# Attention and two gated layers on one core: the first batch's heads in another order, its loads and copies spread over engines, other paces, and idle products on TensorE

## The chip, the cores and the metric

The kernel runs on one core of a Trainium2 chip (trn2). The metric is the device time of one execution in microseconds. The core's engines are TensorE (PE, its weight loads are PEld), VectorE (DVE), ScalarE (ACT), GpSimd (POOL) and SyncE (SP), which issues most DMAs.

## The reference

```python
def _attn_ref(q, k, v):                       # 4 batches, 8 heads, 576 rows, 64 columns
    scores = scale * np.matmul(q, k.transpose(0, 1, 3, 2))
    rel = pos[:, None] - pos[None, :]
    mask_local = (rel >= 0) & (rel < 32)      # heads 0 to 3
    mask_strided = (rel >= 0) & (pos[None, :] % 32 == pos[:, None] % 32)   # heads 4 to 7
    ...
    return np.matmul(softmax(scores), v)

def _moe_ref(x, w_gate, w_val, w_out, rms_g): # x: 2304 x 512, w_gate and w_val: 512 x 1536
    xn = x / sqrt(mean(x * x) + 1e-6) * rms_g
    g = xn @ w_gate
    return (g / (1 + exp(-g)) * (xn @ w_val)) @ w_out
```

The heads of the attention are joined to x (2304 x 512), `_moe_ref` follows with its scale by the root mean square, and a second layer of the same kind without that scale ends it. All arrays are float32.

## The kernel before, in words

**Attention.** A batch (`batch`, L606) is cut into ten groups, each with scores, softmax, a turn of the probabilities and the product with v. Five are *strided* (heads 4 to 7, rows of equal remainder modulo 32, 126 or 108 rows to a group), five are *local* (heads 0 to 3, windows of 64 queries with 96 keys). q and k are loaded with rows on the partitions (`load`, L267) and must be turned on PE (`strided_t`, `local_t`, `local_rest`) before scores can be made; PSUM results are copied to SBUF by ACT, or with `eng()` (L236) by DVE once in a hundred. The local q is written into a zeroed tile `qT`, two heads on a block diagonal (`diagonal`, L316); POOL sets that tile to zero (L310). In `softmax_step` DVE takes the masked row maximum (L397, tile `e` with its maximum `nb`), ACT the exponential (L406), DVE the reciprocal `rc` (L417), and POOL multiplies (L423).

**The way to the first layer.** Outputs go to `x`: ACT squares them, DVE adds the squares to `ss` (`squares`, L535). `rms_step` (L556) sums `ss` over partitions on PE with a tile of ones, DVE takes the mean, POOL the power -0.5 (`rstd`, L576), DVE puts it on a diagonal (`dg`, L581), PE spreads it to all partitions (L587), DVE scales x (L592). Each batch has two parts, of 256 and 320 rows. `split_x` splits x into a rounded part `xh` (ACT) and the rest `xl` (DVE).

**The gated layers.** A product of two float32 matrices is three products of such parts. For each of 12 chunks of the inner dimension there are a gate, a value and a down product (`gate`, `down`). The first layer runs over seven blocks of tokens with chunks 0 to 5, one with all, then the rest (`segs`, L775). Weights come as float32 in 512 KB loads into three buffers (`raw`, L163) and are split by six operations a half kilobyte wide: on ACT L173, L174 and L187, on DVE L180, L181 and L192. Six chunks have 18 such loads, so 54 operations on ACT and 54 on DVE.

**What sets the order.** The program calls `point()` at fixed places: in a loop ahead of the first layer, and behind every half of a gate, value or down product. Each point moves all started steps on by a phase and then starts new ones by `pace`: so many attention steps (`att`) and weight steps (`dec`) to a point. A scheduler then orders each engine's instructions by priorities; every engine runs its own list in order. Ahead of the first layer PE's banks are shared by eight tags, later the attention has two, `a0` and `a1`.

```python
    pace.update(att=1.0)
    for i in range(1000):
        if (0, 0) in att.done:
            break
        pace["dec"] = 0.7 if i >= 0 else 0.0
        point()
```

Ahead of the first layer batch 0 is computed: all strided turns first, then the strided groups, then the local ones; its first scale is started behind the seventh group, its second behind the tenth. The attention of batch 1 is started between the products of the first two token blocks.

Of the kernel before, what the change touches and what calls it, by code (L numbers as in the profile page):

```python
# [25 lines left out]
def attn_ffn_ffn(ctx: ExitStack, tc: tile.TileContext, q, k, v, w1g, w1v, w1o, rms_g, w2g, w2v, w2o, out):  # L26
# [179 lines left out]
    class Attention:  # L206
# [29 lines left out]
        def eng(self):  # L236
            self.turn += 1
            return nc.scalar if self.turn % 100 else nc.vector

        def consts(self):  # L240
# [5 lines left out]
            for m, lead in ((self.m0, 0), (self.m1, 32)):  # L246
                g.memset(m, 0.0)
                for par in range(2):
                    sel(m[64 * par:64 * par + 64], [[-1, 96]], lead, 1)
                    sel(m[64 * par:64 * par + 64], [[1, 96]], 31 - lead, -1)  # L250
# [7 lines left out]
        def load_strided(self, t, src, b, engs=None):  # L258

            engs = engs or [nc.sync] * 5  # L260
            for h in range(HH):
                s = src[b, HH + h].rearrange("(t r) d -> t r d", r=32)[:, 0:30, :].rearrange("t (a g) d -> a t (g d)", g=5)
                engs[h].dma_start(out=t[0:108, h].rearrange("p (g d) -> p g d", d=D), in_=s)  # L263
            s = src[b, HH:H].rearrange("h (t r) d -> t h r d", r=32)[:, :, 30:32, :].rearrange("t h r d -> t h (r d)")
            engs[4].dma_start(out=t[108:126, :, 0:2 * D], in_=s)

        def load(self, b, half):  # L267
            res = []
            for nm, src in (("q", q), ("k", k)):
                if half == 0:  # L270
                    t = self.p1.tile([128, 5, HH * D], F32, tag=nm, name=f"{nm}n{b}{half}")
                else:
                    t = self.p1.tile([126, HH, 5 * D], F32, tag=nm, name=f"{nm}n{b}{half}")
                    self.load_strided(t, src, b, [nc.sync,nc.sync,nc.gpsimd,nc.gpsimd,nc.sync] if b == 0 and nm == "k" else None)
                res.append(t)
            self.ld[b, half] = res
            if half == 0:
                for h in range(0, HH, 2):
                    for t, src in zip(res, (q, k)):
                        for h_ in (h, h + 1):  # L280
                            nc.sync.dma_start(out=t[:, 0:4, h_ * D:(h_ + 1) * D], in_=src[b, h_, 0:512].rearrange("(c p) d -> p c d", p=128))
# [59 lines left out]
        def local_rest(self, b):  # L341
# [9 lines left out]
            def post():  # L351
# [4 lines left out]
                if b + 1 < B:  # L356
                    self.load(b + 1, 1)
# [557 lines left out]
```

## Time and profile before

| | us |
|---|---|
| median of 3 runs | 1068.74 (1063.17 to 1069.88) |
| the profiled execution | 1067.38 |
| its span, first to last instruction | 1065.6 |
| PE busy | 1036.2 (97%) |
| DVE, ACT, POOL busy | 463.8, 438.2, 58.4 |
| moved by DMA | 100.39 MB, 94 GB/s on average |

The profiled execution is one run of the program with the hardware profiler on; durations below are of this execution. Its mean granted TensorE clock was 0.973 of full speed. A busy PE is not PE at its best: at half clock it is as busy and does half the work.

### The profile page before, as it was taken

What the parts mean: (1) busy time and instruction counts of PE and PEld (TensorE: products, weight loads), DVE (VectorE), ACT (ScalarE), POOL (GpSimd) and SP (SyncE); (2) the same over time, 40 slices, a digit from 0 to 9 for tenths busy, and PEclk for the clock granted to TensorE, in tenths of its full rate; (3) what the DMA queues carried; (4) which work ended last, traced back from release to release, by engine and by line L of the source; (5) the groups of instructions that cost most, each with busy time, mean ns of one, the idle gap of its engine ahead of it and who ended that gap; (6) DMA issues with size and microseconds to landing.
All of it is one profiled execution on the core that took longest, in us unless ns stands there. A gap on an engine that the chain in (4) does not pass through costs nothing.

```text
span 1065.6 us, 15758 instructions
## 1 busy us (share of the span) xinstructions
PE 1036.2 (97%) x6056; PEld 912.0 (86%) x6056; DVE 463.8 (44%) x1152; ACT 438.2 (41%) x1082; POOL 58.4 (5%) x83
## 2 busy tenths in 40 slices
PE   4988999999999999999999999999999999999998
PEld 4768999999999999988888898888888888888887
DVE  3788446355455861762313586222224313222212
ACT  5987546645635751651211565222124312212111
POOL 3312102102100000000000000000000000000000
PEclk9658999999999999999999999999999999999999
DMA  7794142243024630642123375111112003030202
GB/s 196 191 242 152 62 124 84 73 113 76 26 77 155 220 132 2 203 165 73 40 60 94 105 249 176 39 40 40 40 40 92 8 1 108 1 99 1 79 1 90
DMA packets 104261, 100.39 MB, mean 94 GB/s; under 512 B 40565, under 2 KB 92477, under 8 KB 103545
## 3 DMA queue, kind: packets, MB, share of 16 engines
q1 hardware_dynamic: 103992, 99.10, 30.2%
q8 instruction: 48, 0.79, 0.3%
q0 software_dynamic: 192, 0.28, 0.1%
q14 instruction: 29, 0.23, 0.1%
HBM read 77.47 MB, written 21.89 MB: 93 GB/s over the span
## 4 chain that ended last, share of the span: by engine, by line
PE 91%; DMA 3%; ACT 3%; DVE 2%; SPq 1%; issue 1%; DVEq 0%; ACTq 0%
PE b_y L63 28%; PE b_a L63 27%; PE b_v L63 17%; PE b_g L63 16%; PE b_a L66 2%; DMA xf<-x_d 1%; SPq L263 1%; DMA raw<-in_moe_w_val_dram 1%; DMA raw<-in_moe_w_gate_dram 1%; ACT e L406 1%; ACT dh L173 0%; DMA raw<-in_moe_w_out_dram 0%; ACT x L73 0%; DVE x L592 0%; DVE dr L180 0%
## 5 line engine op out<-in xcount | busy, mean ns | idle before, releaser
L63 PE MATMUL b_a<-xh,w 128*128 128x512 f32 (+3 forms) x816 | 231.4, 359 | 0.0
L63 PE MATMUL b_g<-xh,w 128*128 128x512 f32 (+3 forms) x696 | 192.6, 342 | 0.7 <-DVE sg L665 0.7
L63 PE MATMUL b_v<-xh,w 128*128 128x512 f32 (+3 forms) x696 | 192.4, 341 | 0.0
L63 PEld LDWEIGHTS b_a<-xh,w 128*128 128x128 f32 x816 | 147.4, 188 | 21.5
L63 PE MATMUL b_y<-hh,w 128*128 128x320 f32 (+3 forms) x624 | 165.1, 329 | 0.0
L675 ACT CAST hh<-sg 128x512 fp32r<-128x512 f32 (+3 forms) x138 | 72.6, 526 | 203.8 <-DVE sg L674 181.4
L63 PE MATMUL b_a<-xl,w 128*128 128x512 f32 (+3 forms) x408 | 146.6, 359 | 0.0
L63 PEld LDWEIGHTS b_g<-xh,w 128*128 128x128 f32 x696 | 125.3, 191 | 13.8 <-DVE sg L665 0.9
L63 PEld LDWEIGHTS b_v<-xh,w 128*128 128x128 f32 x696 | 124.8, 190 | 12.7 <-issue 0.7
L63 PE MATMUL b_y<-w,hh 128*128 128x512 f32 x432 | 133.2, 390 | 0.0
L63 PEld LDWEIGHTS b_y<-hh,w 128*128 128x128 f32 x624 | 110.0, 188 | 8.1 <-issue 0.7
L63 PE MATMUL b_g<-xl,w 128*128 128x512 f32 (+3 forms) x348 | 116.9, 336 | 0.0
L63 PE MATMUL b_v<-xl,w 128*128 128x512 f32 (+3 forms) x348 | 116.5, 335 | 0.0
L674 DVE TENSOR_TENSOR sg<-sg,b_v 128x512 f32<-128x512 f32 (+3 forms) x51 | 31.2, 611 | 167.6 <-PE b_v L63 163.9
L676 DVE TENSOR_TENSOR hl<-sg,hh 128x512 fp32r<-128x512 f32 (+3 forms) x138 | 80.8, 585 | 47.6 <-ACT hh L675 46.7
L674 DVE TENSOR_TENSOR sg<-sg,b_a 128x512 f32<-128x512 f32 (+3 forms) x51 | 31.2, 611 | 160.1 <-PE b_a L63 160.0
L63 PE MATMUL b_y<-hl,w 128*128 128x320 f32 (+3 forms) x312 | 100.8, 323 | 0.0
L63 PEld LDWEIGHTS b_y<-w,hh 128*128 128x128 f32 x432 | 80.4, 188 | 16.2
L667 ACT ACTIVATE sg<-b_a 128x512 f32<-128x512 f32 (+3 forms) x51 | 27.3, 536 | 144.8 <-PE b_a L63 144.7
L63 PEld LDWEIGHTS b_a<-xl,w 128*128 128x128 f32 x408 | 76.8, 188 | 10.9
L63 PE MATMUL b_y<-w,hl 128*128 128x512 f32 x216 | 84.0, 389 | 0.0
L667 ACT ACTIVATE sg<-b_g 128x512 f32<-128x512 f32 (+3 forms) x51 | 27.4, 537 | 121.7 <-PE b_g L63 121.7
(124 smaller groups left out, 1294.6 us busy)
## 6 DMA issues: line engine op xcount, KB each, us to landing
raw<-in_moe_w_gate_dram SPq DMA_DIRECT2D x24, 512.0 KB
raw<-in_moe_w_val_dram SPq DMA_DIRECT2D x24, 512.0 KB
raw<-in_moe_w_out_dram SPq DMA_DIRECT2D x24, 512.0 KB
xf<-y_d SPq DMA_DIRECT2D x5, 1024.0 KB
out_dram<-ob SPq DMA_DIRECT2D x18, 256.0 KB
xf<-x_d SPq DMA_DIRECT2D x8, 512.0 KB
part<-ob SPq DMA_DIRECT2D x14, 256.0 KB
ob<-part SPq DMA_DIRECT2D x14, 256.0 KB
```

Source lines behind the costliest of these rows:

```text
L63: traced(nc.tensor.matmul(out_, a, b_, start=start, stop=stop))
L66: traced(nc.tensor.transpose(out_, a, one))
L263: engs[h].dma_start(out=t[0:108, h].rearrange("p (g d) -> p g d", d=D), in_=s)
L406: r = nc.scalar.activation(out=e[:qn, i, :kn], in_=e[:qn, i, :kn], func=AF.Exp, bias=nb[:qn, i:i + 1], scale=-1.0, accum_out=sums[:qn, i:i ...
L667: last["act"] = ins_of(nc.scalar.activation(out=s[:, :n], in_=pg[:, :n], func=AF.Silu))
L674: nc.vector.tensor_tensor(out=s[:, :n], in0=s[:, :n], in1=pv[:, :n], op=ALU.mult)
L675: last["act"] = ins_of(nc.scalar.copy(out=hh[:, :n], in_=s[:, :n]))
L676: last["dve"] = ins_of(nc.vector.tensor_tensor(out=hl[:, :n], in0=s[:, :n], in1=hh[:, :n].bitcast(F32), op=ALU.subtract))
```

## The change

- **Loads.** For batch 0 the local q and k are loaded first, q by SP and k by ACT's queue, each in one 512 KB load in which a partition holds four neighbouring rows of a head, plus a load of the last 64 rows. Later batches take the same row order with four loads as before. Local v of a batch is loaded in two DMAs in place of nine, and a window's look-back for the first window comes from the head before it, where the mask hides it; `m0` and `kT` have 32 columns more of padding for that. A strided tensor is loaded in seven DMAs of 18 partitions and four heads, in place of four of 108 partitions and one of 18; none is issued by POOL now. One weight load is issued among the first strided loads.
- **Order.** Batch 0 has local groups before strided ones. Its strided turns are started after three groups, its strided q and k have tiles of their own (in weight buffers of chunks not yet loaded). Both scales of batch 0 stand behind all ten groups. The loads of batch 1 follow the strided turns of batch 0.
- **Turning.** In batch 0 the local q and k are turned by products with the identity (64 output rows, one head each), eight to a bank in place of four transposes.
- **Copies.** Ahead of the first layer `eng()` gives copies to DVE and ACT in turn. The first `qT` is zeroed by DVE.
- **Idle products.** `warm(n)` makes n products of ones with the identity into a bank that nobody reads: 8 behind the sums of the first scale, 12 behind its spreading.
- **Paces.** Ahead of the first layer `dec` is 0.25 a point, with one weight step started at once; in the layer `att` is 0.35, 1.1, 0.7, 0.7, 0.65 by blocks, where it was 0.7, 0.7, 0.65.

```diff
         def eng(self):
             self.turn += 1
-            return nc.scalar if self.turn % 100 else nc.vector
+            return nc.vector if state["start"] and self.turn % 2 else nc.scalar
...
+        def load_strided(self, t, src, b, eng):
+            rows = src[b, HH:H].rearrange("h (t r) d -> t h r d", r=32)
+            for a in range(6):
+                eng.dma_start(out=t[18 * a:18 * a + 18], in_=rows[:, :, 5 * a:5 * a + 5, :].rearrange("t h r d -> t h (r d)"))
+            eng.dma_start(out=t[108:126, :, 0:2 * D], in_=rows[:, :, 30:32, :].rearrange("t h r d -> t h (r d)"))
...
+                eng = nc.scalar if b == 0 and i and not half else nc.sync
...
+                    eng.dma_start(out=m_.rearrange("p (h c) -> p h c", h=HH), in_=src[b, 0:HH, 0:512].rearrange("h (p c) d -> p h (c d)", c=4))
...
-                    nc.gpsimd.memset(t, 0.0)
+                    (nc.gpsimd if b else nc.vector).memset(t, 0.0)
...
+                    if b == 0:
+                        for par in range(2):
+                            product(tp[64 * par:64 * par + 64, 128 * c:128 * c + 128], src[0][:, c, 2 * pair + par, :], self.ident,
+                                    start=True, stop=True)
+                    else:
+                        turned(tp[:, 128 * c:128 * c + 128], src[0][:, c, 128 * pair:128 * pair + 128], self.ident)
...
+        def warm(self, n):
+            t = self.abank()
+            for _ in range(n):
+                product(t[:, 0:128], self.ones, self.ident, start=True, stop=True)
...
             def mean():
+                if b == 0 and part == 0:
+                    self.warm(8)
...
             def post():
+                if b == 0 and part == 0:
+                    self.warm(12)
...
+            if b == 0:
+                groups = groups[5:] + groups[:5]
...
+            if b == 0:
+                res += [self.rms_step(b, part) for part in range(2)]
...
+    att.load(0, 0)
+    wq += [weight_step(m, c, z) for m, c in order for z in range(3)]
+    att.load_v(0, 0)
+    start(wq.pop(0))
     att.load(0, 1)
     att.load_v(0, 1)
...
-        pace["dec"] = 0.7 if i >= 0 else 0.0
+        pace["dec"] = 0.25
...
-        pace["att"] = (.7,.65,.65)[min(si // 2, 2)]
+        pace["att"] = (.35, 1.1, .7, .7, .65)[min(si, 4)]
```

PE's list from the sums of the first scale (`ones,ss`) to the first gate product (`b_g<-xh`); `dg,ones` is the spreading of a scale, `ident,qn` and `ident,kn` are turns of batch 1, `kT,qT` its first scores. Before:

```order
L63 MATMUL b_y_806<-ones,ss 128x1 x2
L66 MATMUL b_a_891<-ident,qn_492 128x108 x4
L63 MATMUL b_g<-dg,ones 128x128 x2
L63 MATMUL b_a_896<-ones,ss 128x1 x2
L63 MATMUL b_a_896<-ones,ss 64x1
L66 MATMUL b_a_901<-ident,kn_498 128x108 x4
L66 MATMUL b_a_913<-ident,qn_492 64x108 x4
L66 MATMUL b_a_923<-ident,kn_498 64x108 x4
L63 MATMUL b_a_941<-kT_889,qT_882 126x126 x4
L63 MATMUL b_g<-xh,w_0_0_207 128x256
```

and of the changed kernel the same stretch:

```order
L63 MATMUL b_a_780<-ones,ss 128x1 x2
L63 MATMUL b_g<-ident,ones 128x128 x8
L66 MATMUL b_a_875<-ident,qn_362 128x108 x4
L63 MATMUL b_a_884<-ones,ss 128x1 x2
L63 MATMUL b_a_884<-ones,ss 64x1
L63 MATMUL b_v<-dg,ones 128x128 x2
L63 MATMUL b_y_814<-ident,ones 128x128 x12
L66 MATMUL b_a_889<-ident,kn_370 128x108 x4
L66 MATMUL b_a_905<-ident,qn_362 64x108 x4
L66 MATMUL b_a_917<-ident,kn_370 64x108 x4
L63 MATMUL b_a_936<-kT_873,qT_865 126x126 x4
L63 MATMUL b_g<-xh,w_0_0_225 128x256
```

The eight idle products stand ahead of the spreading, the twelve behind it, with three turns and four scores of batch 1 between them and the gate.

DVE's list from the diagonal of the first scale (`dg`) to the first `xl`; `dr`, `dh` and `w` are weight operations, and the rows with `gcol` scale x. Before:

```order
L581 TENSOR_SCALAR dg<-ident,rstd 128x128 x2
L553 TENSOR_TENSOR ss<-ss,sq 128x320
L181 SCALAR_TENSOR_TENSOR dh<-dh,dr 128x512
L192 TENSOR_TENSOR w_2_2_455<-dh,w_2_2_455 128x512
L592 SCALAR_TENSOR_TENSOR x_761<-x_761,gcol,b_g 128x256 x2
L592 SCALAR_TENSOR_TENSOR x_413<-x_413,gcol,b_g 128x256 x2
L180 SCALAR_TENSOR_TENSOR dr<-raw,dr 128x512
L573 TENSOR_SCALAR mean<-b_a_896 64x1
L573 TENSOR_SCALAR mean<-b_a_896 128x2
L192 TENSOR_TENSOR w_3_0_485<-dh,w_3_0_485 128x512
L180 SCALAR_TENSOR_TENSOR dr<-raw,dr 128x512
L689 TENSOR_TENSOR xl<-x_761,xh 128x256 x2
```

and changed:

```order
L628 TENSOR_SCALAR dg<-ident,rstd 128x128 x2
L180 SCALAR_TENSOR_TENSOR dr<-raw,dr 128x512
L181 SCALAR_TENSOR_TENSOR dh<-dh,dr 128x512 x2
L192 TENSOR_TENSOR w_3_0_737<-dh,w_3_0_737 128x512
L620 TENSOR_SCALAR mean<-b_a_884 64x1
L620 TENSOR_SCALAR mean<-b_a_884 128x2
L180 SCALAR_TENSOR_TENSOR dr<-raw,dr 128x512
L641 SCALAR_TENSOR_TENSOR x_448<-x_448,gcol,b_v 128x256 x2
L641 SCALAR_TENSOR_TENSOR x_679<-x_679,gcol,b_v 128x256 x2
L192 TENSOR_TENSOR w_3_1_777<-dh,w_3_1_777 128x512
L628 TENSOR_SCALAR dg<-ident,rstd 128x128 x2
```

Between the diagonal and the scaling of x stand five weight operations now, where there were two.

POOL's list of batch 1's strided groups (126 and 108 rows), with the memset of that batch's `qT`. Before:

```order
L423 TENSOR_TENSOR e<-e,rc 126x4x126
L310 MEMSET qT_1193 128x2304
L423 TENSOR_TENSOR e<-e,rc 126x4x126
L423 TENSOR_TENSOR e<-e,rc 108x4x108 x3
L423 TENSOR_TENSOR e<-e,rc 128x4x96 x4
```

and changed:

```order
L457 TENSOR_TENSOR e<-e,rc 126x4x126 x2
L457 TENSOR_TENSOR e<-e,rc 108x4x108 x2
L330 MEMSET qT_1316 128x2304
L332 MEMSET kT_1360 128x32
L457 TENSOR_TENSOR e<-e,rc 108x4x108
```

The memset has moved from behind the first group to behind the fourth.

## Rows read from the trace of the kernel before

**Rows 1.** The page's 40 slices: PE's busy tenths, the granted clock's tenths.
```profile
PE   4988999999999999999999999999999999999998
...
PEclk9658999999999999999999999999999999999999
```

**Rows 2.** Four stretches of the span: busy us of each engine (instructions).
```profile
core 0: us, PE busy (x) PEld busy (x) DVE busy (x) ACT busy (x) POOL busy (x), PEclk, DMA share, GB/s
0.00:69.45 69.45, 48.94 (x317) 39.12 (x317) 45.47 (x157) 55.13 (x168) 20.44 (x39) 0.70 0.82 211
69.45:100.00 30.55, 26.97 (x155) 24.27 (x155) 25.08 (x85) 23.15 (x73) 7.38 (x6) 0.72 0.68 196
100.00:1000.00 900.00, 898.96 (x5251) 795.32 (x5251) 378.24 (x885) 350.27 (x821) 30.54 (x38) 1.00 0.26 85
1000.00:1065.60 65.60, 61.34 (x338) 53.29 (x336) 14.99 (x27) 9.61 (x20) 0.00 (x0) 1.00 0.16 56
```

**Rows 3.** PE in order of time: start us, us, instruction, [idle before <- releaser].
```profile
8.69 1.07 PE L66 MATMUL b_a<-ident,qn 126*128 126x126 f32 x4 [8.69 <-DMA qn<-in_q_dram]
...
60.03 1.22 PE L63 MATMUL b_g<-dg,ones 128*128 128x128 f32 x4 [1.23 <-DVE dg L581]
61.05 1.15 PE L63 MATMUL b_a<-ones,ss 128*128 128x1 f32 x6
...
67.45 2.07 PE L63 MATMUL b_a<-kT,qT 64*126 64x126 f32 x8 [0.65 <-ACT qT L73]
69.45 0.58 PE L63 MATMUL b_g<-xh,w 128*128 128x256 f32 x1
...
90.38 1.10 PE L66 MATMUL b_a<-ident,e 126*126 126x126 f32 x4 [2.21 <-POOL e L423]
```

**Rows 4.** Five stretches of PE: length, busy (instructions), granted clock, DMA.
```profile
69.45:82.90 13.45, 13.45 (x57) 0.50 0.89 232
82.90:88.30 5.40, 5.26 (x42) 1.00 0.79 256
88.30:90.40 2.10, 0.02 (x1) 0.84 0.54 191
90.40:93.20 2.80, 2.80 (x14) 0.51 0.01 3
93.20:100.00 6.80, 5.44 (x46) 1.00 0.51 157
```

**Rows 5.** DVE in order of time: the first maximum, the first xl.
```profile
16.02 0.29 DVE L397 CUSTOM_DVE_ANT_0 e<-b_y,ms 126x126 f32<-126x126 f32 x1 [16.02 <-PE b_y L63]
...
65.45 0.75 DVE L689 TENSOR_TENSOR xl<-x,xh 128x256 fp32r<-128x256 f32 x2
```

**Rows 6.** The stretch between these two, columns as in rows 2.
```profile
16.02:65.45 49.43, 39.78 (x268) 31.22 (x265) 41.47 (x147) 46.65 (x153) 14.89 (x15) 0.62 0.91 220
```

**Rows 7.** SP's first issues, and two stretches (columns as in rows 2).
```profile
0.74 3.30 SPq L263 DMA_DIRECT2D qn<-in_q_dram  x4
...
8.00:12.00 4.00, 2.22 (x10) 1.88 (x11) 0.00 (x0) 0.61 (x2) 0.00 (x0) 1.00 0.43 148
16.00:20.00 4.00, 1.76 (x28) 1.59 (x25) 3.58 (x30) 3.09 (x13) 2.02 (x1) 1.00 1.14 340
```

**Rows 8.** DVE groups to 110 us (busy, mean), and L180: min/median/max ns.
```profile
L75 DVE COPY qT<-b_a 64x512 f32<-64x512 f32 x3 | 2.1, 694 | 0.1
L75 DVE COPY qT<-b_a 64x128 f32<-64x128 f32 x1 | 0.3, 295 | 0.3 <-ACT qT L73 0.3
...
L180 DVE SCALAR_TENSOR_TENSOR dr<-raw,dr x18: 675/688/1395, 18.2 to 93.8; 128x512 uint32<-128x512 uint32 x18
```

**Rows 9.** POOL in order of time, batch 1's memset and what follows.
```profile
87.32 2.02 POOL L310 MEMSET qT<- 128x2304 f32 x1 [8.34 <-PE b_a L63]
89.30 3.20 POOL L423 TENSOR_TENSOR e<-e,rc 126x504 f32<-126x504 f32 x3
```

More of the change, by code (lines that the diff above doesn't have):

```diff
@@ L373, in post @@
                 o = (0, 504, 936)[part]
-                copy(self.eng(), self.qk_tile(b, 1, which)[:m, o:o + 4 * n], cell["t"][:m, 0:4 * n])
+                copy(self.eng(), self.strided_qk(b, which, o, 4 * n)[:m], cell["t"][:m, 0:4 * n])
                 self.count(b, 1)
-                if last:
+                if last and b:
                     self.load(b, 0)
-                    if b == 0:
-                        self.load_v(0, 0)
+                elif last:
+                    self.load(1, 1)
             return Step([pe, post])
@@ L506, in mms @@
                     o = self.SOFF[g] + h * n
[L507 removed]
+                    product(bank_[:n, 128 * h:128 * h + n], self.strided_qk(b, 0, o, n)[row], self.strided_qk(b, 1, o, n)[row],
+                            start=True, stop=True)
                 return bank_
@@ L547, in squares @@
                     x = self.x_tile(b, 0)
-                    rest = [(x[:, a, o:o + n], self.ss[b][:, o:o + n]) for a in range(2)]
+                    if b == 0:
+                        nc.scalar.activation(out=ss[:, o:o + n], in_=x[:, 0, o:o + n], func=AF.Square)
+                    rest = [(x[:, a, o:o + n], ss[:, o:o + n]) for a in range(int(b == 0), 2)]
                 for xa, sa in rest:
@@ L600, in store @@
                 self.done.add((b, part))
-            return Step([wait] * 3 + [pe1, mean, diag] + [wait] * 1 + [bc, post, store], lambda: (b, part + 1) in self.sq and (not part or (b, 0) in self.done), PRIO_R, "r")
+            return Step([wait] * 3 + [pe1, mean, diag] + [wait] * 1 + [bc, post, store], lambda: {(b, 0), (b, part + 1)} <= self.sq and (not part or (b, 0) in self.done), PRIO_R, "r")
         TILES = [tuple((p, j) for j in js) for js in ((0, 1, 2, 3), (4, 5, 6, 7)) for p in range(2)] + [((0, 8), (1, 8))]
@@ L798, in attn_ffn_ffn @@
     make_identity(nc, att.ident)
+    att.load(0, 0)
+    wq += [weight_step(m, c, z) for m, c in order for z in range(3)]
+    att.load_v(0, 0)
+    start(wq.pop(0))
     att.load(0, 1)
     att.load_v(0, 1)
-    wq += [weight_step(m, c, z) for m, c in order for z in range(3)]
-    for _ in range(0):
-        start(wq.pop(0))
     att.consts()
```

127 lines of the change are left out of this document (70 added, 57 removed).

## The prediction

> **What bounds the kernel now.** I read the page first, then the windows over the whole span, then the start in finer views. The page [rows 1] shows TensorE at 9 tenths or more in all but the first four slices, and in exactly these the granted clock is 9, 6, 5 and 8 tenths. The four stretches [rows 2] say it in numbers: from 100 us to 1000 us PE stands idle 900.00 - 898.96 = 1.04 us at clock 1.00, and in the last 65.60 us it idles 4.26 us on the way of the last results. So from 100 us on the time is TensorE's own work, which the change hardly touches, and only what lies before 100 us can be won or lost.
>
> The first product of the gated layers starts at 69.45 us [rows 3]. Between there and 100 us PE gets through less work than it could, in two ways [rows 4]. 13.45 us run at clock 0.50, the lower of the two levels (1.2 GHz), and 2.80 us more at 0.51: at 2.4 GHz these would be 6.73 and 1.40 us. And PE idles: 0.14, 2.08 and 1.36 us. In work at the full clock the stretch holds 6.73 + 5.26 + 0.02 + 1.40 + 5.44 = 18.85 us in 30.55 us, so 11.70 us are lost, 8.1 of them to the clock and 3.6 to waits.
>
> If F is the time at which the first gate product starts, this gives one formula for the new span: F + 18.85 + 965.60 + r = F + 984.45 + r, where r is what is still lost behind F. Before it is 69.45 + 984.45 + 11.70 = 1065.6, the span. The profiled execution took 1067.38 us, 1.78 more than its span, and 0.13% under the median of the three runs, 1068.74. A measurement of this kernel can tell about 1%, 10.7 us, from no change; faster by that means under 1058.05.
>
> What sets F: from the first row maximum on DVE at 16.02 us to the first low part of x (xl) at 65.45 us [rows 5], DVE is busy 41.47 us of 49.43, ACT 46.65, PE 39.78 [rows 6]. ACT is the tightest, PE is slow because its clock is 0.62 there, and DVE has 8 us of room.
>
> **The change part by part.**
>
> *First loads.* The first product waits for q until 8.69 us [rows 3]; SP spends 3.30 us on issuing four strided heads [rows 7]. Now one 512 KB load of q goes out first on SP and one of k on ACT beside it, in runs of 1 KB as the weights have them. With the strided loads alone in flight the core moved 148 GB/s, with weights in flight 340 [rows 7]. 1.05 MB at 340 is 3.1 us; issue until about 1.6 and some 2 us to landing, as in the first product of before, give about 6.5 us for both tensors. The Trainium skill (Trainium Kernel Development and Optimization, Key Constraints) speaks against a gain by the second queue: loads issued from SP, ACT and POOL run on the same 16 DMA engines, and issuing from several saves the issue time alone. The 340 GB/s were fed by SP's queue alone, which agrees; by the opposite, two queues at 340 each, q and k would be there 1.5 us earlier and the time 1.5 us shorter.
>
> The local q and k of the first batch now lie four neighbouring rows to a partition, so each pair needs 8 products with the identity instead of 4 transposes. At half clock two such products take 1.02 us to the next instruction [rows 3], 0.51 each, so 0.26 at full clock, which is what the trace grants up to 20 us. 32 of them are 8.3 us; with one set of edge turns, the copies behind them and the first scores, about 16 us for the first maximum, as before. Starting 2 us earlier is used up by the dearer turning.
>
> *Copies.* Up to the first high part of x, ACT loses 17 of its 40 PSUM copies and gains 3 weight operations. On DVE, between the first maximum and the first xl, stand 15 copies now, 3 before. Copies of 512 and 128 elements took 694 and 295 ns on DVE [rows 8], 1.04 ns an element and 162 ns: 3 of 512, 3 of 504, 3 of 432, one of 256, 2 of 126 and 3 of 108 make 7.8 us, less 1.7 for the three of before, +6.1. Four more weight operations at 0.69 (the median [rows 8]) are +2.8, three more small ones of the scale +0.7. An operation overlaps the next by about 0.1 us, which takes 2 off for these 19. DVE's busy time from maximum to xl is then 41.5 + 6.1 + 2.8 + 0.7 - 2 = 49.1, say 49.5, where it had a stretch of 49.43 with ACT full. DVE takes over as the tightest engine; ACT has room. Given the idle time that the tightest engine had before (49.43 - 46.65 = 2.8), the first xl comes at 16 + 49.5 + 2.8 = 68.3, later than before by 3. Bounds: without idle time and without POOL's disturbance (L180 takes 1395 ns at worst against 688 [rows 8]; over the stretch an excess of some 4 us) 61.5; with twice the idle time and a late start 73.
>
> *Memset of qT on DVE* for the first batch, 2.02 us on POOL before: it lies ahead of the first copy, when DVE waits for loads. Nothing hangs on it; uncovered it would cost 2.
>
> *Idle products.* 8 and 12 of 0.51 us at half clock, 0.26 at full: 4.1 and 6.1, or 2.1 and 3.1 us. The order shows them on PE around the broadcast of the first scale. Queued behind them are the broadcast (only behind the 8), three turns of the next batch and its first scores (0.9 to 2.1 us each at half clock [rows 3]), then the first gate product. DVE needs scale, one weight operation, one of the scale and two more before the first xl. At full clock the 12 products, three turns (1.5) and scores (1.0) end with that; at half clock they are some 5 us late. Before, PE's low clock put 4.0 us between first xl and first gate product; now I take 1.2, so F = 69.5, where it was.
>
> *The clock.* Before, PE ran at 0.50 until 82.9, after 15 us without a pause, in which products of 64 rows alternate with the gates, and then rose; after the pause at 88.3 it rose again 2.8 us after work of 128 rows began [rows 4]. The idle products have 128 rows and 128 columns, and with the broadcast they fill the 10 us before F without long pauses. I take the clock as full from F on, or very near it: the 8.1 us go.
>
> *Paces.* While the first token block runs, 0.35 instead of 0.7 attention steps start at each point, and 1.1 in the second block. The pause of 2.21 us at 90.38 waited for POOL's normalising [rows 3], which stood behind POOL's 2.02 us memset of the next qT [rows 9]. That memset is issued later now, after four of five strided groups, and there are fewer attention steps in the block. But DVE stays dense there, 25 us of 30.55 [rows 2], so waits will not all go. Of the 3.6 us of waits and the 1.4 that followed at the low clock I leave half: r = 2.5.
>
> *Weights, later batches, the end.* Fourteen weight loads are issued ahead of the first store of x, as against thirteen, and at the first gate product some 18 of the 54 weight operations of the first six chunks remain on DVE, as before. Later batches issue fewer local v loads; with PE idle 1.04 us in 900 that is hidden. The end is untouched.
>
> **Sum.** 69.5 + 984.45 + 2.5 = 1056.45, plus 1.78: 1058 us, 10.7 under the median, on the edge of what can be told.
>
> **Rivals.**
>
> A. As forecast, 1053 to 1063: 0.45.
>
> B. DVE is less tight: local heads' short softmax lets POOL work at other times, and DVE neither idles nor is disturbed. First xl 61.5, F = 62.7: 62.7 + 984.45 + 2.5 + 1.78 = 1051. For it: ACT and PE leave room. Against it: before, the tightest engine idled 2.8 us. 0.25.
>
> C. The idle products do not raise the clock, or their place is so early that it falls again: the 6.7 us of the first half-clock stretch stay lost, 1065. For it: 15 us of work before 82.9 did not raise it at once. Against it: the second rise within 2.8 us. 0.15.
>
> D. The strided loads, now of 18 partitions, come late; PE's queue has the strided turns ahead of the first local probabilities, so all wait. At 148 GB/s q and k strided (1.15 MB) take 7.8 us, behind 0.88 MB of v at 5.9 us; all end near 22 us where PE wants them at 17. F moves by 5: 1063. The Trainium skill (DMA: Bandwidth & Descriptors, Why a DMA increments its semaphore by 16 and not by 1) says a load runs on the largest number of engines up to 16 that divides the slowest dimension of both sides: 6 before (108 and 6), 9 now (18 and 18); an estimate by it is 148 x 9 / 6 = 222 GB/s, 5.2 us, and the wait would go. The 148 against 340 fits that rule, so 0.08.
>
> E. Slower: 1.1 steps a point in the second block start more softmax chains than POOL and DVE follow; PE meets an unfinished normalising. One such wait cost 2.2 us and 1.4 at the low clock, 3.6 together [rows 3, 4]. Slower by 1% needs 1079.4, so six such waits or more: 1058 + 21.6 = 1080. Against it: at 0.65 to 0.7 there was 1.04 us of idle in 900, and ACT and DVE have room once the weights are done. 0.07.
>
> **How the numbers follow.** The likeliest is A, 1058. The range reaches from below B, with a first maximum 3 us early, to 1070 through C with a part of E: 1048 to 1070. Faster: all of B and half of A, 0.48. Slower: E, 0.07. The rest, 0.45, within 1%.
>
> **What would show it.** Right: first gate product at 66 to 73 us, granted clock 1.00 in the 10 us behind it, DVE's idle time between first maximum and first xl below 5 us and ACT's above it, PE idle from F to 100 us below 3 us and near 1 us later. Wrong: a first gate product before 64 (B), clock 0.50 behind it (C), PE waiting for strided q or k near 20 us (D), or waits for POOL's normalising between 100 and 150 us (E).

## The result and the profile after

The changed kernel took 1074.56 us (median of 20 runs, 1068.68 to 1079.42), the kernel before 1066.59 (20 runs beside it). The ratio is **1.0075, 95% interval 1.0055 to 1.0094**: slower by three quarters of a per cent, where 1058 and a gain were forecast.

The 20 runs lie in two groups, nine at 1068.7 to 1071.8 and eleven at 1073.7 to 1079.4; their mean granted clock is 0.979 to 0.984 in the nine and 0.971 to 0.978 in the eleven. The groups are not sharply apart: two of four later runs took 1072.36 and 1072.82 us. The first trace is of the quicker group (1069.75 us, span 1067.8), a second trace of the unaltered kernel, taken with the experiments, is of the other (1078.03, span 1075.9). Both are needed below.

By the formula of the prediction the span is F + 984.45 + r, with F the start of the first gate product. The page's slices of the first trace, and PE in order of time (columns as in [rows 3]):

```profile
PE   6868999999999999999999999999999999999998
...
PEclk9769999999999999999999999999999999999999
```

```profile
17.91 0.62 PE L66 MATMUL b_a<-ident,qn 126*128 126x126 f32 x4 [0.28 <-DMA kn<-in_k_dram]
...
21.56 0.62 PE L66 MATMUL b_a<-ident,kn 126*128 126x126 f32 x4 [2.59 <-DMA vs<-in_v_dram]
...
59.01 3.76 PE L63 MATMUL b_g<-ident,ones 128*128 128x128 f32 x16
...
64.37 2.84 PE L63 MATMUL b_y<-ident,ones 128*128 128x128 f32 x24
68.59 0.59 PE L66 MATMUL b_a<-ident,kn 108*128 108x108 f32 x4 [1.38 <-ACT qT L73]
...
73.31 0.93 PE L66 MATMUL b_a<-ident,kn 108*64 108x108 f32 x4 [3.76 <-ACT kT L73]
74.17 2.06 PE L63 MATMUL b_a<-kT,qT 64*126 64x126 f32 x8
76.16 0.58 PE L63 MATMUL b_g<-xh,w 128*128 128x256 f32 x1
```

and the start of the gate in the second trace:

```profile
83.28 0.58 PE L63 MATMUL b_g<-xh,w 128*128 128x256 f32 x1
```

F is 76.16 (69.45 in [rows 3]), and r = 1067.8 - 76.16 - 984.45 = 7.2 (11.7 before). In the second trace F is 83.28 and r = 1075.9 - 83.28 - 984.45 = 8.2. So the way to F lost 6.7 or 13.8 us, and 4.5 or 3.5 came back behind it. The rows also show a wait of 2.59 us ahead of the first turn of the strided k (`kn`) at 21.56, the idle products (`ident,ones`, counted twice each) at 59 and 64 us, and two pauses between them and F. The row at 21.56 names a load of v (`vs`), which SP issues behind k; the turn itself reads k alone. The clock rises under the products and is gone again before F (stretches of PE: length, busy, granted clock):

```profile
62.90:69.90 7.00, 5.27 (x46) 0.99 0.60 217
69.90:80.10 10.20, 6.79 (x28) 0.50 0.94 224
80.10:100.00 19.90, 16.84 (x129) 1.00 0.61 207
```

The way itself, from the first row maximum on DVE to the first xl, answers to [rows 6]; first trace, then second trace, busy us of PE, PEld, DVE, ACT and POOL in each stretch, then the granted clock:

```profile
core 0: us, PE busy (x) PEld busy (x) DVE busy (x) ACT busy (x) POOL busy (x), PEclk, DMA share, GB/s
14.27:72.87 58.60, 44.03 (x316) 36.19 (x316) 45.52 (x167) 45.87 (x145) 11.83 (x15) 0.74 0.72 195
20.00:40.00 20.00, 18.28 (x142) 14.60 (x142) 11.37 (x51) 13.97 (x53) 5.59 (x6) 0.81 0.80 222
40.00:60.00 20.00, 13.38 (x84) 10.20 (x85) 19.77 (x56) 17.97 (x50) 3.33 (x4) 0.59 0.69 171
60.00:72.87 12.87, 8.17 (x59) 7.71 (x58) 9.26 (x23) 8.48 (x18) 2.08 (x4) 0.77 0.67 205
```

```profile
13.06:79.95 66.89, 51.97 (x316) 42.38 (x316) 45.47 (x166) 45.94 (x145) 12.22 (x15) 0.62 0.68 174
20.00:40.00 20.00, 19.08 (x104) 15.78 (x104) 11.29 (x50) 10.09 (x37) 4.16 (x5) 0.50 0.82 213
40.00:60.00 20.00, 16.36 (x104) 11.78 (x103) 12.84 (x42) 14.46 (x47) 4.77 (x6) 0.59 0.45 102
60.00:79.95 19.95, 12.35 (x79) 11.16 (x78) 16.21 (x38) 14.75 (x33) 2.46 (x4) 0.67 0.78 205
```

DVE's work is the same in both, 45.5 us; its idle time is 13.1 in one and 21.4 in the other (8.0 in [rows 6]). Between 20 and 40 us PE is the full engine, and DVE idles 8.6 and 8.7 us. PE is full at a reduced clock: in the first trace it falls to 0.50 at 22 us, returns at about 25.5 and falls again just before 36, with PE busy all the while; in the second it is 0.50 until 52, though PE works without a gap from 20.9 to 47. PE alone in four stretches, first trace and second trace:

```profile
core 0: us, PE busy (x), PEclk, DMA share, GB/s
24.00:28.00 4.00, 4.00 (x34) 0.81 1.04 334
28.00:32.00 4.00, 4.00 (x42) 1.00 0.63 177
32.00:36.00 4.00, 4.00 (x40) 0.97 0.68 177
36.00:40.00 4.00, 3.84 (x20) 0.50 0.86 240
```

```profile
24.00:28.00 4.00, 4.00 (x23) 0.50 0.98 336
28.00:32.00 4.00, 4.00 (x30) 0.50 0.61 164
32.00:36.00 4.00, 4.00 (x18) 0.50 0.61 140
36.00:40.00 4.00, 4.00 (x24) 0.50 1.09 240
```

DVE's longest wait there is for the last turn of the local heads' probabilities (`b_g`, L66), which stands on PE's list behind local products and strided scores. First trace, then second:

```profile
39.88 0.42 DVE L75 COPY pT<-b_g 96x256 f32<-96x256 f32 x1 [4.38 <-PE b_g L66]
```

```profile
47.09 0.42 DVE L75 COPY pT<-b_g 96x256 f32<-96x256 f32 x1 [7.38 <-PE b_g L66]
```

These two rows stand 7.2 us apart and the first gate products 7.1: what parts the two traces is over by then.

What DVE waits for at the end of the way (first trace, DVE in order of time):

```profile
60.99 0.69 DVE L180 SCALAR_TENSOR_TENSOR dr<-raw,dr 128x512 uint32<-128x512 uint32 x1 [1.04 <-ACT dr L174]
...
65.62 0.69 DVE L180 SCALAR_TENSOR_TENSOR dr<-raw,dr 128x512 uint32<-128x512 uint32 x1 [2.53 <-ACT dr L174]
...
68.94 1.64 DVE L641 SCALAR_TENSOR_TENSOR x<-x,gcol,b_v 128x256 f32<-128x256 f32 x4
...
72.87 1.41 DVE L740 TENSOR_TENSOR xl<-x,xh 128x256 fp32r<-128x256 f32 x4
```

The broadcast of the scale is done by 64.5. The scale of x (L641) starts at 68.94, because weight operations stand ahead of it on DVE and one of them waits for ACT's dr, the part of a weight that ACT's L174 makes. On ACT that one waits for a weight load:

```profile
64.91 0.67 ACT L174 ACTIVATE dr<-raw 128x512 uint32<-128x512 uint32 x1 [3.09 <-DMA raw<-in_moe_w_val_dram]
```

### The profile page after: what moved, and what is told of

Same layout as the page of the kernel before. It is cut to its first block, busy times and chain, and to the rows that moved or that the text cites. A ratio compares the mean times of both kernels' runs of the same rounds, so it can differ in the third digit from the quotient of the medians.

```text
span 1067.8 us, 15950 instructions
## 1 busy us (share of the span) xinstructions
PE 1037.0 (97%) x6144; PEld 914.1 (86%) x6144; DVE 473.2 (44%) x1169; ACT 441.0 (41%) x1067; POOL 53.9 (5%) x89
## 4 chain that ended last, share of the span: by engine, by line
PE 88%; DMA 4%; DVE 4%; ACT 1%; SPq 1%; issue 1%; POOL 0%; DVEq 0%; ACTq 0%; POOLq 0%
PE b_y L63 27%; PE b_a L63 27%; PE b_g L63 16%; PE b_v L63 16%; PE b_a L66 2%; DMA raw<-in_moe_w_gate_dram 1%; DMA xf<-x_d 1%; DVE x L641 1%; DMA qn<-in_q_dram 1%; DMA part<-ob 0%; DVE dr L180 0%; DMA x_d<-x 0%; DVE xl L740 0%; DMA raw<-in_moe_w_val_dram 0%; SPq L305 0%
## 5 line engine op out<-in xcount | busy, mean ns | idle before, releaser
L727 DVE TENSOR_TENSOR hl<-sg,hh 128x512 fp32r<-128x512 f32 (+3 forms) x138 | 81.8, 593 | 49.5 <-ACT hh L726 48.7
```

The costliest lines, as they stand in the source:

```text
L727: last["dve"] = ins_of(nc.vector.tensor_tensor(out=hl[:, :n], in0=s[:, :n], in1=hh[:, :n].bitcast(F32), op=ALU.subtract))
```

## The experiments

Three theories: **L**, the weight operations with late loads ahead of the scale set F; **V**, VectorE has too much work; **K** (with **C**), PE's clock sets it. Where an expectation gives a letter another meaning, or brings a new one, it says so. Five sets of kernels, each set beside its own runs of before.

**The changed kernel once more.** Measured 1072.36 to 1078.03 in 4 runs, ratio 1.0095 (1.0069 to 1.0122).

> The changed kernel once more, unaltered, for a second trace beside those of the experiments. Its 20 times so far lie in two groups, 1069 to 1072 us and 1074 to 1079. Theory L (late loads: the weight operations of ScalarE and VectorE that stand ahead of the scale of x wait for loads of the weights, and the first gate product is late by that) expects the first gate product at 76 +- 1 us in this trace too, with a VectorE wait of 2 to 3 us for ScalarE's dr some 10 us before it. Theory V (VectorE has taken too many copies and is simply full) expects no wait of VectorE over 1 us between 55 us and the scale. If the profiled run belongs to the slower group, theory C (the clock) expects the granted clock to rise some 6 us or more later behind the first gate product, and everything before it to stand within 1 us of the first trace.

The trace was of the other group: F 83.28, not 76, and what precedes it was not within 1 us: DVE waited 7.38 us for PE before 47.09. L's wait for ACT's dr is there, 3.55 us before 72.70. C was wrong on the place: these two traces part ahead of F, between 20 and 47 us.

**Scale first.** The weight operations of the fourth chunk and later are held back, and those of DVE ordered behind the scale:

```diff
-        for st in list(active):
+        for st in [s for s in active if not (state["start"] and len(s) <= 4 and getattr(s, "late", 0))]:
...
+                    if (b, part) == (0, 0): last["dve"] = ins_of(r)
```

> The changed kernel, with the weight operations of the fourth chunk and later held until the scale of x has been emitted, and their VectorE part ordered behind it: on VectorE the scale now stands behind the diagonal products alone, no L180 that waits for a load is ahead of it. Theory L: scale at 64.5 us (it was 68.9), casts xh at 67 to 68, first gate product at 71 to 72.5 us (it was 76.2), the time 1061 to 1066 us, 4 to 8 below the changed kernel's quicker runs. Theory V: VectorE has the same work, so the first gate product stays at 75 to 77 us and the time at 1069 to 1078. Theory C (only the clock behind the first gate product costs): the first product may be earlier, but what is left behind it grows by as much, time 1068 or more.

Six runs: 1066.15 and 1067.51, then 1072.46 to 1075.2; ratio 1.0059 (1.0028 to 1.0089). In the trace (1066.15) the scale comes where L said and F a little sooner, but no run is below 1066. DVE's and PE's rows of this kernel:

```profile
64.13 1.66 DVE L641 SCALAR_TENSOR_TENSOR x<-x,gcol,b_v 128x256 f32<-128x256 f32 x4 [0.37 <-PE b_v L63]
```

```profile
70.58 0.38 PE L63 MATMUL b_g<-xh,w 128*128 128x256 f32 x1
...
77.42 0.39 PE L63 MATMUL b_g<-xh,w 128*128 128x256 f32 x1 [1.44 <-DVE sg L716]
...
83.90 0.38 PE L63 MATMUL b_g<-xh,w 128*128 128x256 f32 x1 [2.21 <-DVE sg L716]
```

L holds for F: 5.6 us earlier than in the first trace, with nearly its clock from 20 to 40 us (0.78 and 0.81). But r rose from 7.2 to 1064.3 - 70.58 - 984.45 = 9.3: PE then waits for DVE's sg. And shorter and longer runs remain, so L doesn't explain these. Here the pauses behind the idle products are 0.61 and 0.68 us, and the clock is 1.00 from F to 80 us.

**Loads of v later.** Moving the calls that load the second batch's v behind the store of x:

> The changed kernel, with the loads of the second batch's v (seven strided ones and two local ones) issued behind the first store of x instead of ahead of the weight loads; the order on VectorE and ScalarE is the same. Theory L: the load of the fourth chunk's gate weights lands by 58.5 us (it was 60.3) and that of its value weights by 61.5 (it was 64.9), the 2.5 us wait of VectorE and the 3.1 of ScalarE go, first gate product at 71 to 73 us, the time 1061 to 1067. Theory V: first gate product unchanged at 76 us, time 1069 to 1078. If the second batch's strided scores then wait for their v, TensorE shows waits for vs between 80 and 130 us, and some of it comes back.

1069.49 to 1078.7, 1.0091 (1.0059 to 1.0122), F 74.52. On SP's queue the strided v loads were still issued at 53.84 us, where they had been, and ACT still waited 3.08 us. The edit did not move what it should, so nothing follows, and why that weight load is late stays open.

**No idle products**, both calls taken out:

> The changed kernel without its 8 and 12 idle products (they write a bank that nobody reads, so the result is the same). Theory C, in the form that the clock falls back during TensorE's pause at 70 us whatever they do: first gate product at 75.5 to 76.5 us, granted clock 0.50 in the 4 us behind it as now, time 1069 to 1078, no change. What I had predicted of them, that they save 8 us of half clock, would give 1077 or more here with the clock at 0.50 until 85 us or later. If they delay the chain (the broadcast behind the first 8), the first gate product comes 1 to 3 us earlier.

1071.13 to 1077.3, 1.0101 (1.0077 to 1.0126) beside 1.0095 for the changed kernel: no difference that shows. The trace (1075.73) has the clock at 0.50 from 20 to 40 us, as the second trace has, so F is not the 76 expected but 82.07, beside 83.28 with the products. They bring nothing here that shows.

**Idle products where k is late**, and the same with the scale first:

```diff
+                if (b, which, part) == (0, 1, 0): self.warm(10)
                 cell["t"] = tp = self.abank()
```

> The changed kernel with ten more idle products on TensorE just behind the first turned strided q, where it stood idle for 2.6 us (18.9 to 21.5) until the strided k had come. In the first trace of the changed kernel the granted clock fell there and came back 3 us later; in the second it fell a little earlier and stayed at 0.50 until the idle products at 70 us, with the first gate product 7.1 us later. Theory K (this pause decides between the two groups of runs): the granted clock is 1.00 from 0 to 34 us in the trace, the first gate product at 75 to 76.5 us, and all runs lie at 1066 to 1072, none at 1074 or above. If the groups come from something else (the chip, a later pause), some of the runs still lie at 1074 to 1079.

> The same ten idle products together with the weight operations held behind the scale of x. Theory K with theory L: first gate product at 70 to 71.5 us in every run and all runs at 1062 to 1067, within 2 us of the kernel before. If VectorE's supply of the gate and value products bounds what is behind (theory V: it was 4.0 us late for sg in the changed kernel, and more, 4.3 in the run with the scale first), the 5 us of an earlier first product are given back in part: 1064 to 1067 rather than 1060 to 1063. Theory without K: two groups of runs stay, at 1066 and 1073.

Alone: 1067.38 to 1075.41 in 12 runs, 1.0041 (1.0018 to 1.0065). The trace has PE at full clock to 36 us, DVE fuller between 20 and 40, and F at 70.38. Its row (columns as above):

```profile
20.00:40.00 20.00, 18.60 (x172) 15.38 (x172) 15.48 (x73) 16.27 (x62) 5.59 (x6) 0.93 0.83 219
```

So much for K in one trace; but four of the 12 runs are above 1073, two of them above the 1074 that K excluded, and the edit also changed the order of PE's turns behind the products, so the clock's share is not separated. With the scale first too: 1070.51 to 1076.99, 1.0056 (1.0034 to 1.0078), F 74.57, where 70 to 71.5 was expected; the clock fell at 31 us after another pause, of 2.37 us. The two gains did not add up.

**The strided loads in their former form**, four transfers over 108 partitions and one over 18:

> The changed kernel with the strided loads (q, k, v; both batches) as before in their form: four transfers over 108 partitions and one over 18, instead of six over 18 and one over 18, in the changed order and all on SyncE's queue. Theory D (the form over 18 partitions brings k late): TensorE's wait for k falls from 2.6 us to under 1, the granted clock stays at 1.00 until 30 us or later, all runs at 1064 to 1071. If it is their place in the queue (issued behind the local loads and a weight load), the wait for k is the same 2 to 4 us or longer, and the runs still lie in two groups.

Ten of 12 runs at 1068.82 to 1070.85, the others 1075.32 and 1078.64; 1.0037 (1.0013 to 1.006). The wait for k did not shrink, it was 3.05 us (2.59 with the new form), and F was 75.44. So the new form is not what makes k late. From 16 to 22 us strided loads alone are in flight (length, PE's clock, DMA share, GB/s; new form, then former):

```profile
16.00:22.00 6.00, 1.00 0.62 169
```

```profile
16.00:22.00 6.00, 0.78 0.44 147
```

That k's place behind the local loads makes it late is the expectation's other reading, but no run moved it. With the former paces too (below) five of 12 runs were above 1073, so it isn't shown that the form changes the groups either.

**Copies back on ScalarE**, on the kernel with ten products and the scale first:

> The run with ten idle products and the scale first, and in addition the copies of the way to the first scale given back to ScalarE, as they were before the change. Theory V (VectorE has taken too much): VectorE's share between 40 and 60 us falls from 9.9 of 10 to about 8.5, the first gate product comes at 68 to 70 us, the time is 2 to 4 us below the run with the copies shared. Theory L (the copies shared are right, ScalarE was the tighter engine before): ScalarE is busy 9.8 of 10 there, the first gate product 2 to 4 us later, 73 to 75, and the time 2 to 4 us above.

1076.49 to 1079.61, 1.0098 (1.0068 to 1.0129): slower than its base by some 5 us, F 80.03. V, which had this kernel faster, falls for the way to F. But ACT was not at 9.8 of 10, as this expectation's L had it:

```profile
40.00:60.00 20.00, 19.58 (x118) 14.13 (x118) 13.19 (x44) 16.37 (x56) 5.59 (x5) 0.50 0.28 78
```

PE is the full engine from 40 to 60 us, at half clock, and DVE and ACT both have room. In this one trace the loss has PE's place, not ACT's; what the copies and what the clock did to it is not separated.

**Single parts on the kernel before**: shared copies; the idle products; the later paces; and shared copies, idle products and the weights' pace of 0.25 together.

```diff
-            return nc.scalar if self.turn % 100 else nc.vector
+            return nc.vector if state["start"] and self.turn % 2 else nc.scalar
...
+                    self.warm(8)
...
+                    self.warm(12)
...
-        pace["att"] = (.7,.65,.65)[min(si // 2, 2)]
+        pace["att"] = (.35, 1.1, .7, .7, .65)[min(si, 4)]
```

> The kernel before with one part of the change alone: on the way to the first scale every other copy goes to VectorE. ScalarE was busy 9.7 to 10 of 10 us there from 20 us on in the kernel before, and giving the copies back to it in a variant of the changed kernel cost about 5 us. Theory S (the shared copies are a gain, what loses is elsewhere): first gate product at 65 to 67 us, the time 2 to 4 us below before. Theory V (VectorE becomes the bound): first product at 69 to 72, the time the same or up to 2 us above.

> The kernel before with the 8 and 12 idle products alone, at the same two places of the first scale. My prediction's step: granted clock 1.00 in the 10 us behind the first gate product, which saves up to 8 us of half clock: 1058 to 1062. Theory C (the clock falls again in the pauses that follow, and what is left behind the first product then waits for VectorE's sg): the first product at 69 to 71, the time within 2 us of before.

> The kernel before with the changed paces of the attention of later batches alone (0.35, 1.1, 0.7, 0.7, 0.65 by block). My prediction's step: half of 3.6 us of waits goes, 1065 to 1066 against 1067. The rival in which POOL's normalising becomes late in the second block: 1075 or more. If these paces are what makes the changed kernel slower: 1069 or more with no change before the first gate product.

> The kernel before with three parts of the change: shared copies, idle products, and the weights' pace of 0.25 on the way to the first scale, but strided heads first, its own loads and its own later paces. If the new order of the heads and their loads is what makes the changed kernel slower (theory O: it makes TensorE wait for the strided k, its clock falls, and VectorE idles 9 us between 20 and 40 us), this kernel is faster than before: 1057 to 1063, first gate product at 64 to 67 us. If the pace of the weights is what costs, it is 1068 or more, with VectorE or ScalarE waiting for loads of weights ahead of the scale.

| part on the kernel before | ratio (95%) | F, us |
|---|---|---|
| shared copies | 1.0034 (1.0009 to 1.0058) | 72.00 |
| idle products | 1.0014 (0.9992 to 1.0036) | 72.89 |
| later paces | 1.0040 (1.0016 to 1.0064) | 69.88 |
| copies, products, weights' pace | 1.0017 (0.9989 to 1.0044) | 72.20 |

None is a gain that shows. Two cost by themselves, 0.34 and 0.40%, together as much as the whole change, but parts don't add up: with the shared copies and two more parts the kernel is at 1.0017, and undoing the paces in the changed kernel (below) leaves 1.0057. S is wrong on the kernel before: with shared copies PE is busy 18.9 of the 20 us from 40 to 60, at 0.50, and DVE 13.9. The idle products again: PE of that kernel around them, then the clock in three stretches up to and behind F.

```profile
62.48 2.84 PE L63 MATMUL b_y<-ident,ones 128*128 128x128 f32 x24
65.16 0.54 PE L66 MATMUL b_a<-ident,qn 108*128 108x108 f32 x4
...
70.90 2.06 PE L63 MATMUL b_a<-kT,qT 64*126 64x126 f32 x8 [1.29 <-ACT qT L73]
72.89 0.58 PE L63 MATMUL b_g<-xh,w 128*128 128x256 f32 x1
```

```profile
61.80:68.80 7.00, 5.36 (x48) 0.97 0.89 266
68.80:72.89 4.09, 2.80 (x15) 0.53 1.12 334
72.89:85.90 13.01, 13.01 (x54) 0.50 0.80 226
```

The clock does rise with the products and is lost again before F, in the pauses of the second batch's turns; the gate products behind F run at 0.50 for 13 us, as in [rows 4]. And the turn behind the twelve products has to wait for them, 2.7 us from 62.48 to 65.16: from the first xl to F it is 6.7 us here, 4.0 in the kernel before.

The later paces make the kernel before slower with F as it was, as the third branch of the expectation has it. They gave no wait for POOL between 100 and 150 us. Behind that PE idled, and lost the clock for a while (the trace, 1073.38 us):

```profile
100.00:150.00 50.00, 50.00 (x443) 47.23 (x441) 21.34 (x84) 26.96 (x87) 4.61 (x7) 1.00 0.23 70
150.00:200.00 50.00, 48.87 (x352) 45.65 (x350) 24.29 (x115) 27.73 (x103) 9.72 (x10) 0.86 0.37 104
200.00:300.00 100.00, 97.32 (x828) 91.38 (x827) 46.87 (x194) 55.44 (x187) 14.61 (x18) 0.98 0.23 63
```

**Parts undone in the changed kernel**: the later paces; these and the strided form; and each of the two further edits on top.

> The changed kernel with the paces of later batches' attention as before (0.7, 0.65, 0.65 for two blocks each). On the kernel before, the changed paces alone cost 0.40% (0.16 to 0.64). If they cost as much in the changed kernel (theory P): 3 to 5 us less, the quicker group at 1065 to 1068, and TensorE's waits between 100 and 300 us (1.4 us of idle time in the changed kernel) under 1 us. If they cost only where the blocks begin earlier: no change, groups at 1069 to 1072 and 1074 to 1079.

> The changed kernel with two parts undone: the strided loads in their former form (which alone gave 1068.8 to 1070.9 in ten of twelve runs) and the former later paces. Theory P, and the parts add up: 1064 to 1067 in most runs, level with before. If the new order of heads with its late k is what loses (theory O): 1068 to 1071 as without the paces, first gate product at 75 us.

> The same as the run with the strided loads' form and the paces undone, and ten idle products where TensorE waits for k. Theory K (the clock between 20 and 34 us): granted clock 1.00 to 34 us, first gate product at 70 to 72 us, time 1060 to 1064, below before. Otherwise the first product stays at 74 to 76 us, or VectorE and the loads of weights take up the gain: 1066 to 1070.

> The same as the run with the strided loads' form and the paces undone, and the weight operations of the fourth chunk held behind the scale of x. Theory L: first gate product at 70 to 72 us, 4 to 5 earlier than without, time 3 to 5 below it, 1060 to 1063. If what is held back is missing behind the first product (TensorE waits for VectorE's sg and for the weights of the fourth chunk between 75 and 110 us): no more than 2 us below it.

| kernel | ratio (95%) | F, us |
|---|---|---|
| later paces as before | 1.0057 (1.0031 to 1.0083) | 75.69 |
| and strided form as before | 1.0061 (1.0033 to 1.0088) | 74.82 |
| and ten products at k | 1.0059 (1.0037 to 1.0080) | 79.26 |
| or the scale first | 1.0056 (1.0023 to 1.0089) | 70.02 |

P is not borne out: the runs of the first two kernels begin at 1068.8 and 1067.05, above what P had, and in the changed kernel undoing the paces removes PE's idle time between 150 and 300 us but leaves 3.45 us between 300 and 500 (1.26 with the new ones). K's forecast for the third kernel failed: the clock was 0.50 from 32 to 40 us, behind another pause of 2.37 us, and F 79.26.

Theory O fits best, but only in part. The second kernel of this table and the last of the table above have the same shared copies, idle products, weights' pace, strided form and later paces; they differ in the new order of heads and what goes with it (local loads and turns, the forms and queues of loads, the place of both scales, the sums of squares, q's memset on DVE, one early weight load). Their ratios differ by 0.0044, some 4.7 us; with their half widths taken as independent, by 0.5 to 8.8 us. So this group of parts costs time. Against O: without them the kernel was to take 1057 to 1063 with F at 64 to 67, and it took 1068.9 in the median with F at 72.20. And some of the difference lies far behind F: PE idles 3.42 us between 300 and 500 us in the one trace, 0.73 in the other.

What the new order does on the way to F shows in all traces. With it, and without products added at k, DVE idles 8.0 to 8.9 us between 20 and 40 us (ten traces); with the former order 1.0 to 4.1 us (six). The clock alone does not do that: it was 0.50 to 0.81 in the ten, and 0.57 in the kernel before, where DVE idled 4.1 us.

The last kernel says most about what stands behind F. F is 70.02 and the clock full from there on, nearly as I had forecast, and still the profiled run takes 1068.91 (r = 1067.1 - 70.02 - 984.45 = 12.6):

```profile
70.02:100.00 29.98, 23.49 (x179) 20.59 (x178) 29.01 (x92) 27.65 (x81) 9.64 (x7) 1.00 0.73 211
```

PE idles 6.49 of 29.98 us here, with DVE at 9.7 of 10 and ACT at 9.2, and 4.39 us more from 100 to 1000 us (1.04 in [rows 2]).

**Less work for VectorE.** The last operation of the output weights of six chunks goes to GpSimd:

```diff
-                nc.vector.tensor_tensor(out=t[:, 1], in0=cell["h"], in1=t[:, 0].bitcast(F32), op=ALU.subtract)
+                (nc.gpsimd if z == 2 and m == 1 and c < 6 else nc.vector).tensor_tensor(out=t[:, 1], in0=cell["h"], in1=t[:, 0].bitcast(F32), op=ALU.subtract)
```

> The run with the scale first (strided form and later paces as before), and the last operation of the output weights of the first six chunks on GpSimd instead of VectorE: six operations of about 0.6 us less on VectorE before some 115 us. Theory V2 (behind the first gate product VectorE's amount of work is the bound): TensorE's idle time between 80 and 100 us falls from 5.9 to about 3, the time is 2 to 4 us below the run without, about 1064 to 1065 in its quick runs. If GpSimd is then late for the softmax or holds VectorE back: same or slower, with TensorE or VectorE waiting for GpSimd.

> The kernel before with the same six operations on GpSimd. Theory V2: TensorE's 3.6 us of waits between 80 and 100 us shrink by half or more, 1064 to 1066 in the profiled run, 1 to 3 us below before. If ScalarE (9.7 to 10 of 10 us busy from 20 to 60 us) is the bound of the way there: no change ahead of the first gate product and within 1 us of before in all.

1.0064 (1.0040 to 1.0088) on the scale first, against 1.0056 without; 1.0006 (0.9985 to 1.0026) on the kernel before. V2 finds no support: PE's idle time between 80 and 100 us did not fall, it was 6.1 us on the scale first (5.9 without) and 5.0 on the kernel before (3.6 without), and the times change by nothing that can be told. GpSimd takes 1.28 us for each in the median, DVE 0.68. Whether DVE and ACT bound the stretch together is left open; taking work off both was not tried. No kernel here is shown to be faster than the one before.

## Why the prediction was wrong

The forecast of F was 16 + 49.5 + 2.8 + 1.2 = 69.5. Measured in the first trace, step by step: first maximum 14.27, busy 45.52, idle 13.08, from first xl to F 3.29, together 76.16. In the second: 13.06, 45.47, 21.42, 3.33, together 83.28. Against the kernel before, F of the first trace is 6.7 us later: 4.1 of it more work on DVE and 5.1 more idle time, less 1.8 and 0.7 at the two ends.

- **First loads**: PE starts at 5.95 us (6.5 forecast). The 32 turning products take 6.5 us, not 8.3, so the first maximum comes 1.7 us sooner than the 16 forecast.
- **DVE's busy time** (49.5): 4 us too high. The instructions came nearly as counted, 20 more than the 147 of [rows 6] where 19 were counted, but they add 4.0 us, not 8.
- **The step that failed is the idle time, "given the idle time that the tightest engine had before", 2.8 us.** Measured are 13.08 and 21.42 us. I made DVE the tightest engine of the whole way and costed nothing of PE between 16 and 40 us. From 20 to 40 us PE is the tight one: 18.28 and 19.08 busy of 20 us, DVE with 8.6 and 8.7 idle. PE waits 2.59 and 2.27 us for k, then works through turns, scores and products, at half clock for two stretches of some 4 us in one trace and for all of it in the other, and DVE waits for its last local turn. I did not consider that the clock can cost 7 us of F on this stretch, though [rows 6] has it at 0.62. Between the two traces it is the clock; against the kernel before, with 0.57 between 20 and 40 us, the clock is not the difference, and the new order with what goes with it is, as far as the traces above go.
- **"Four more weight operations at 0.69"** were counted as work alone, with their loads there in time. Two late loads cost 1.04 and 2.53 us of DVE ahead of the scale, a part of the 13.08; holding these operations back gave F 5.6 us earlier.
- **"I take the clock as full from F on"**: wrong, and rival C is what happened, in its form "their place is so early that it falls again". PE pauses 1.38 and 3.76 us behind the products; the clock falls at 69.9 and gate products run at 0.50 until 80.1. From the first xl to F it is 3.29 us, not 1.2, with the last turn and the scores at half clock behind the pause of 3.76. The clock fell the same way with the products alone on the kernel before. Where the pauses were shorter (scale first) the clock stayed, as forecast, and the time gained was lost in part to waits for DVE.
- **r = 2.5**: 7.2. The first 3.94 us behind F at half clock are 2.0 of it, idle time to 100 us is 3.07 (forecast half of 3.6), idle time from 100 to 1000 us is 2.69, 1.65 more than in [rows 2].
- **Rival D** had the right place and half of the size: 2.59 us of waiting for 5. With strided loads alone in flight, 16 to 22 us, the changed kernel moved 169 GB/s at a DMA share of 0.62, with the former form 147 at 0.44. The Trainium skill (DMA: Bandwidth & Descriptors, Why a DMA increments its semaphore by 16 and not by 1) states that a load runs on the largest number of engines up to 16 that divides the slowest dimension of both sides. By it the number rose from 6 to 9, and the prediction's estimate of 222 GB/s took the speed to rise with it. The trace nearly agrees on the number, as the share rose 1.4 times, but the speed rose by 15% only, and "the wait would go" was wrong. What holds the speed is open; SP took 4.27 us to issue six pieces of k, 540 KB, so its issuing is one rival.
- **Rivals B and E**: no F below 64 anywhere. PE waits for no POOL between 100 and 150 us in either trace; the result is on E's side of zero, but not by its mechanism.

F and r account for the span by their definition, so that the sum closes proves nothing; but the work behind F is the same, 5741 PE instructions in the kernel before and in both traces. The sum: F is 6.66 too low, r 4.69, what lies around the span 0.17; 1058.2 and these 11.5 are the 1069.75 of the profiled run. The other group adds 7.1 in F and 1.0 in r.

## What to carry to other kernels

When a change makes one engine lighter and another the tightest, cost every engine in every stretch of the way, not only the one that is full on average: here, in the first trace, the full engine changes from TensorE (20 to 40 us) to VectorE (40 to 60), and then a load holds VectorE up (60 to 66). An earlier start of a stage is not worth its full time where the engines that feed the stage have no room behind it: a first product 5.6 and 4.8 us earlier made the profiled runs 3.6 and 0.8 us shorter. And look at the waits behind idle products before placing them: here the clock they had raised was lost in a pause of 3.76 us, and in another kernel in pauses of 0.88, 0.76 and 1.29 us, before the work that they were meant for.

## What was not expected of the hardware

- The same instructions in the same order met the clock differently. TensorE worked without a gap from 21.6 to 39.8 us in the first trace and from 20.9 to 47 in the second. In the first it was back at 2.4 GHz at about 25.5 us and at 1.2 GHz again just before 36, with no pause between; in the second it stayed at 1.2 GHz throughout, and F differed by 7.1 us. That this parts all runs of the changed kernel into two groups is likely by their mean clocks, but shown for two traces only; the kernel before has a spread too (1062.24 to 1071.84 in 29 runs of one set).
- Strided loads cut into pieces of 18 partitions, where it was 108, had 1.44 times the DMA share (0.62 against 0.43 in [rows 7]) and moved 1.14 times as much (169 against 148 GB/s).
